# A lead with its mask loaded third, its queries in four loads, and its value sums by streaming columns

## The chip, the cores and the metric

The kernel runs on one core of a Trainium2 chip. The metric is the device time of one execution, in microseconds; of several runs the median is given. A core has TensorE (PE in the profile, its weight loads PEld), VectorE (DVE), ScalarE (ACT), GpSimd (POOL) and SyncE (SP), which here issues all DMAs.

## The reference

Local attention with block summaries, then two feed-forward layers, all in float32:

```python
k_sum = k.reshape(B, H, nb, block, D).max(axis=3)      # B 2, H 8, S 768, D 64; block 32, nb 24
v_sum = v.reshape(B, H, nb, block, D).mean(axis=3)
scores_l = where(|i - j| < 16, q @ k.T / sqrt(D), -1e9)
scores_s = q @ k_sum.T / sqrt(D) + log(block)
a = softmax(concat([scores_l, scores_s]))
x = a @ concat([v, v_sum])                             # -> 1536 x 512
h = relu(x @ w_in);  x = (h * h) @ w_out               # 512 -> 2048 -> 512
h = x @ w_in2;       return silu(h) @ w_out2
```

## The kernel before

Attention is done in 24 tiles of 64 queries (12 for each of the two batches), for all 8 heads at once, two heads to a product. A tile sees 96 keys (its window) and 24 block summaries, so 120 columns. The feed-forward layers split each float32 operand into a high and a low part and multiply three times. The first layer runs over three blocks of 512 tokens, that is of 8 tiles; the first block can start when tiles 0 to 7, the **lead**, are through attention. Tiles 8 to 15 and 16 to 23 go beside the products of the blocks.

In the first block the order of all engines but GpSimd is written by a planner, `first_order` (line 64): a list of operations, each with engine, duration, due time and what it needs. At each step it takes the operation that can start first, and on that engine, of those that can start by then, the one with the smallest due. Loads are ordered by due alone. The durations in it are the author's; the orders that come out are fixed in the program, and each engine then runs its list in that order, waiting where an operand is late.

The names of the lead's operations, which the steps below use:

- `kt`, `q`, `cst`, `vr`, `vl`: loads on SyncE of the keys (4, a head pair each), the queries (2, four tiles each), the mask with an identity matrix, the value rows (3) and the values by windows (2). `raw` loads a chunk of weights.
- `ksum` (VectorE) takes the block maxima of a head pair's keys, `kwl` (ScalarE) and `ksl` (VectorE) copy windows and maxima side by side.
- `psl` (TensorE) makes the scores of one tile and head pair, `ttl` (VectorE, line 441) adds the mask and takes the minimum, `exl` (ScalarE, line 446) the exponential with its sum; `ze`, `rc`, `nt` (VectorE, lines 466 to 477) normalise the tile; `psa` (TensorE, line 483) transposes it, `a` copies it to SBUF: on VectorE for the tiles in AVEC, on ScalarE for the others.
- `vs` (TensorE) sums the value rows in blocks, by six products into one bank, psv: the weights are a 128x24 slice of `share` (1/32 at the rows of a block), the rows stream with 512 columns. `vmean` (ScalarE, twice) copies the 24x512 means from that bank behind the windows of four tiles each (vlead).
- `av` (TensorE) multiplies two tiles' probabilities with their values, `xh` (ScalarE) and `xl` (VectorE) write the high and low part of the result. `highs` and `gemm1` 0 are the first large product; they need all four `xh`, the last also all four `xl`.
- `sc`, `sh`, `st2`, `hi`, `lo` decode a chunk of weights on ScalarE and VectorE.

Dummy matmuls (`turn`, on idle_in) are issued ten at the start (WARM), and behind the scores of tile 3: six after its first head pair, four after its second (`FILL`, line 49). The planner's durations do not count them.

Of the kernel before, what the change touches and what calls it, by code (L numbers as in the profile page):

```python
# [53 lines left out]
NMIXED = 2  # L54
PSS_AT = (1, 5, 9, 13)
PSA_AT = (3, 7, 11, 14)
AVEC = (5, 6, 7)
FIRST2 = 1
DEC1 = 14
LEADX = range(0, NLEAD, 2)  # L60
# [9 lines left out]
def first_order():  # L70
# [6 lines left out]
    def op(eng, name, arg, dur, due, deps=(), bank=(), kb=0):  # L77
        o = index[name, arg] = dict(eng=eng, name=name, arg=arg, dur=dur, due=due + shift.get(name, 0), deps=list(deps), bank=bank, kb=kb,
                                    n=len(ops))
        ops.append(o)  # L80
# [17 lines left out]
        return 24 + 7 * s  # L98


    for i, (name, arg, kb) in enumerate([("kt", 0, 393), ("q", 0, 524), ("kt", 1, 393), ("cst", 0, 250), ("kt", 2, 393),
                                         ("kt", 3, 393), ("q", 1, 524), ("vr", 0, 524), ("vr", 1, 524), ("vr", 2, 524),
                                         ("vl", 0, 1150), ("vl", 1, 1150)]):
        load(name, arg, kb, -100 + i)
    for hp in range(NHP):
        op("vec", "ksum", hp, 1.0, -50 + hp, [("kt", hp, 0)])
# [1 line left out]
            op("act", "kwl", (hp, i), .5, -50 + hp + 51 * i, [("kt", hp, 0)])  # L108
            op("vec", "ksl", (hp, i), .13, -50 + hp + 48 * i, [("ksum", hp, 0)])
    for c in range(6):  # L110
        op("pe", "vs", c, .92, 2.7 + .1 * c, [("vr", c // 2, 0)])
    for i in range(NLEAD // NGRP):
        op("act", "vmean", i, 1.9, -5, [("vs", c, M) for c in range(6)] + [("vl", i, 0)] * 0)
    for i in range(NVF):
        op("act", "vfm", i, .6, tile_due(NLEAD) - 10 + i, [("vmean", 0, 0), ("xh", LEADX[-1], 0)])

# [10 lines left out]
    for g in range(NFIRST):  # L127
        due, two = tile_due(g), g - 2 >= NLEAD
        if g < NLEAD:
            for hp in range(NHP):  # L130
                op("pe", "psl", (g, hp), .29, due, [("kwl", (hp, g // NGRP), A), ("ksl", (hp, g // NGRP), A), ("q", g // NGRP, 0)] +
                   [("psl", (g, hp - 1), 0)] * (hp > 0), bank=[] if hp else [("acc", "ttl", (g, NHP - 1))])
                op("vec", "ttl", (g, hp), .21, due, [("psl", (g, hp), M), ("cst", 0, 0)])
                op("act", "exl", (g, hp), .385, due, [("ttl", (g, hp), A)])
            exp = [("exl", (g, hp), A) for hp in range(NHP)]
        else:
            load("kw", g, 246, due - 9, [pss(g - 2) + (M,)] * two)
            load("qr", g, 131, due - 8.9, [("qd", g - 2, A)] * two)
            load("vf", g, 196, due - 6, [av(g - 2) + (M,)] * two)
            op("vec", "kwc", g, .13, due - .5, [("kw", g, 0)] + [("kvr", 2 * NHP - 1, 0)] * (g >= TPB))  # L140
            if TPB <= g < TPB + NVF:
                op("vec", "vfc", g, .35, due, [("vf", g, 0), ("vendc", 0, A)])
            op("pool", "qd", g, .72, due - 5, [("qr", g, .1)] + [pss(g - 2) + (M,)] * two)
            if g == NLEAD:
                op("pe", "vis", g, 1.95, due, [("gemm1", 1, 0), ("kwc", g, A), ("qd", g, A)], bank=[("att", "ttr", g, g + 1)])
            elif g % 2 == 0:
                op("pe", "vis", g, 3.1, due, values(g - 2) + values(g - 1) + [("kwc", g, A), ("qd", g, A)],
                   bank=[("h", "xl", g - 2), ("att", "ttr", g, g + 1)])
            else:
                index["vis", g - 1]["deps"] += [("kwc", g, A), ("qd", g, A)]  # L150
            op("vec", "ttr", g, .84, due, [pss(g) + (M,)] + [psa(g - 2) + (M,)] * two)
            op("act", "exp", g, 1.54, due, [("ttr", g, -.45)])
            exp = [("exp", g, A)]
        op("vec", "ze", g, .09, due, exp)
        op("vec", "rc", g, .1, due, [("ze", g, .1)])
        op("vec", "nt", g, .78, due, [("rc", g, .1)])
        if g < NLEAD:
            op("pe", "psa", g, .62, due - 2, [("nt", g, -.1)], bank=[("att", "a", g)])
        elif g % 2 == 0:
            op("pe", "psa", g, .85, due - 2, [("nt", g, -.1)], bank=[("att", "a", g, g + 1)])  # L160
        else:
            index["psa", g - 1]["deps"] += [("nt", g, -.1)]
        op("vec" if g in AVEC else "act", "a", g, .65 if g in AVEC else .56, due, [psa(g) + (M,)] + [av(g - 2) + (M,)] * (g >= NLEAD + 2))
        if g < NLEAD and g % 2:
            op("pe", "av", g - 1, 1.15, due, [("vl", g // NGRP, 0), ("vmean", g // NGRP, A), ("a", g - 1, A), ("a", g, A)],
               bank=[("acc", "xl", g - 1)])
            op("act", "xh", g - 1, .6, due, [("av", g - 1, M)])
            op("vec", "xl", g - 1, .7, due, [("xh", g - 1, A)])
        elif g % 2:
            if g == NFIRST - 1:  # L170
                op("pe", "av", g - 1, 1.3, due, values(g - 1) + values(g), bank=[("h", "xl", g - 1)])
            op("act", "xh", g - 1, .6, due, [av(g) + (M - 1.8 * (g < NFIRST - 1),)])
            op("vec", "xl", g - 1, .7, due, [("xh", g - 1, A)])
# [71 lines left out]
def kernel(  # L245
# [32 lines left out]
    def mm(o, l, r, **kw):  # L278
        pe.matmul(o, l, r, **kw)  # L279

    def copy(eng, o, i, scale=1.0):
        if eng is act:
            return act.activation(out=o, in_=i, func=AF.Copy, scale=scale)  # L283
        return eng.tensor_copy(out=o, in_=i)  # L284
# [88 lines left out]


    share_p = ctx.enter_context(tc.tile_pool(name="share_p", bufs=1, side="right"))
    share = share_p.tile([P, PHASE - 8], F32, tag="share", name="share")
    att_ctx = ExitStack()
    cp = att_ctx.enter_context(tc.tile_pool(name="cp", bufs=1, side="right"))
    p1 = att_ctx.enter_context(tc.tile_pool(name="p1", bufs=1, side="right"))
# [14 lines left out]

    pool.memset(share, 0.0)
    for j in range(P // KBLK):
        pool.memset(share[j * KBLK:(j + 1) * KBLK, NSUM - P // KBLK + j:NSUM - P // KBLK + j + 1], 1.0 / KBLK)
    st = {}

    def summaries(b, sums, tag):  # L400
# [234 lines left out]
    def first_block():  # L635
# [3 lines left out]

        idle_in = wi_p.tile([P, 512], F32R, tag="wi", name="idle_in")  # L640
        idle_out = ps_h.tile([P, 512], F32, tag="h", name="idle_out")
        psv = ps_h.tile([P, DM], F32, tag="h", name="psv0")
        vec.memset(idle_in.bitcast(F32), 0.0)
        early = first_p.tile([P, 1], F32, tag="early", name="early")
        act.activation(out=early, in_=idle_in[:, 0:1].bitcast(F32), func=AF.Exp)
# [18 lines left out]
            sp.dma_start(out=kts[hp][:, WIN:], in_=kT[0, hp])  # L664

        def q(i):
            gr = slice(i * NGRP, i * NGRP + NGRP)
            sp.dma_start(out=qrlead[i], in_=qW[gr].rearrange("g e d n -> (e d) g n"))

        def cst_(_):  # L670
            sp.dma_start(out=cst_sb[:, 0:3 * NK + P], in_=cst)
# [35 lines left out]
            turn(FILL.get(ghp, 0))  # L707

        def vs(c):
            lo = NSUM - P // KBLK - c * (P // KBLK)  # L710
            mm(psv[NWIN:NK], share[:, lo:lo + NSUM], vrows[c // 2][:, c % 2], start=(c == 0), stop=(c == S // P - 1))

        def vmean(i):
            means = psv[NWIN:NK]
            copy(act, vlead[NWIN:NK, i * NGRP:i * NGRP + NGRP].rearrange("p g h d -> p g (h d)"),
                 bass.AP(means.tensor, means.offset, [means.ap[0], [0, NGRP], means.ap[1]]))

# [101 lines left out]
        def psa(g):  # L819
            for i in (g,) if g < NLEAD else (g, g + 1):  # L820
                transposes(i)

        do = dict(kt=kt, q=q, cst=cst_, vr=vr, vl=vl, ksum=ksum_, kwl=kwl, ksl=ksl, vs=vs, vmean=vmean, vfm=vfm, kv=kv, kvr=kvr,
                  vend=vend, vendc=vendc, vfc=vfc, kw=kw_load, qr=q_load, vf=v_load, kwc=k_sums, qd=side_by_side,
                  vis=vis, ttr=minima, exp=exps, ze=guard, rc=inverse, psl=psl, ttl=lambda a: minimum(*a),
                  exl=lambda a: exponential(*a), nt=lambda g: norm(g, vec),
# [393 lines left out]
```

## Time and profile before

| | us |
|---|---|
| median of 3 runs | 583.91 (583.61 to 584.04) |
| the profiled execution | 583.73 |
| its span, first to last instruction | 581.9 |
| first large product starts (chain) | 34.91 |
| TensorE busy | 574.5 (99%) |
| VectorE, ScalarE busy | 386.4 (66%), 360.1 (62%) |

The profile is of one execution. Times in it count from the first instruction. Each group of instructions stands with the line of kernel.py that made it, which may be a helper's (279 is the matmul helper, 283 the copy on ScalarE, 284 that on VectorE), so tiles tell more than lines. The granted clock is TensorE's, 1.00 for full speed.

### The profile page before, as it was taken

How to read it: one execution, taken by the hardware profiler on the slowest of the kernel's cores; microseconds unless marked ns; L12 is line 12 of the kernel's file. 1: busy time of each engine (PE TensorE's matmuls, PEld its weight loads, DVE VectorE, ACT ScalarE, POOL GpSimd, SP SyncE). 2: the span in 40 equal slices, each digit the busy share in tenths (PEclk: the TensorE clock that was granted, in tenths of full speed). 3: DMA queues.
4: the chain of work that ended last, by engine and by line, in shares of the span. 5: the costliest groups of instructions: out<-in, count | busy, mean ns of one | idle time of the engine just before them, and what ended most of it. 6: DMA issues, size and time to landing. Idle time of an engine off the chain costs nothing.

```text
span 581.9 us, 9507 instructions
## 1 busy us (share of the span) xinstructions
PE 574.5 (99%) x3300; PEld 489.5 (84%) x3300; DVE 386.4 (66%) x966; ACT 360.1 (62%) x834; POOL 93.0 (16%) x101
## 2 busy tenths in 40 slices
PE   8999999999999999999999999999999999999997
PEld 6578888888888888888888889999988988889995
DVE  5999899953955765286454778666665666666641
ACT  5999878864646545376544677565555655555541
POOL 0010100102654452175332200000000000000000
PEclk9999999999999999999999999999999999999999
DMA  8999989755998879345880111242258411111002
GB/s 317 310 267 330 316 296 333 241 212 168 295 339 289 298 245 364 122 134 160 313 262 2 38 54 73 90 146 90 91 169 338 146 37 37 36 37 37 27 12 108
DMA packets 42240, 104.42 MB, mean 179 GB/s; under 512 B 4560, under 2 KB 11856, under 8 KB 42192
## 3 DMA queue, kind: packets, MB, share of 16 engines
q1 hardware_dynamic: 42192, 103.81, 52.7%
q8 instruction: 26, 0.43, 0.3%
q14 instruction: 22, 0.18, 0.1%
HBM read 78.37 MB, written 25.43 MB: 178 GB/s over the span
## 4 chain that ended last, share of the span: by engine, by line
PE 96%; ACT 2%; DMA 1%; DVE 1%; SPq 0%; issue 0%; DVEq 0%
PE acc L279 45%; PE h L279 23%; PE hx L279 12%; PE hz L279 6%; PE pss L279 3%; PE hy L279 3%; PE psa L483 2%; PE av L279 1%; DMA t_ksum<-in_kT_dram 1%; PE psv L279 1%; ACT vlead L283 1%; ACT T L446 0%; ACT xt L283 0%; PE idle_out L279 0%; DVE ksum L684 0%; DVE T L441 0%
## 5 line engine op out<-in xcount | busy, mean ns | idle before, releaser
L279 PE MATMUL h<-xt,wi 128*128 128x512 f32 x576 | 139.8, 392 | 1.0 <-ACT xt L283 1.0
L279 PE MATMUL acc<-g,wo 128*128 128x512 f32 x576 | 139.5, 391 | 0.0
L279 PE MATMUL acc<-wq,g 128*128 128x512 f32 x576 | 134.3, 390 | 0.0
L279 PEld LDWEIGHTS h<-xt,wi 128*128 128x128 f32 x576 | 107.1, 188 | 23.9 <-ACT xt L283 1.1
L279 PEld LDWEIGHTS acc<-g,wo 128*128 128x128 f32 x576 | 107.6, 188 | 22.6 <-issue 0.5
L279 PEld LDWEIGHTS acc<-wq,g 128*128 128x128 f32 x576 | 107.8, 188 | 21.9 <-DVE wq L287 0.3
L287 DVE TENSOR_TENSOR g<-r,g 128x512 fp32r<-128x512 f32 x48 | 38.8, 807 | 66.0 <-ACT g L283 40.1
L287 DVE TENSOR_TENSOR r_s<-v,r_s 128x256 fp32r<-128x256 f32 x48 | 20.3, 426 | 64.7 <-ACT r_s L283 64.7
L283 ACT ACTIVATE e<-hx 128x384 f32<-128x384 f32 x32 | 15.7, 492 | 60.4 <-PE hx L279 60.4
L446 ACT ACTIVATE T<-T,m 128x120 f32<-128x120 f32 x96 | 36.6, 382 | 7.0 <-DVE m L441 6.9
L283 ACT ACTIVATE g<-s 128x384 fp32r<-128x384 f32 x64 | 32.9, 516 | 10.5 <-DVE s L287 10.4
L279 PE MATMUL hx<-x_t,r_s 128*128 128x384 f32 x192 | 38.5, 335 | 0.0
L287 DVE TENSOR_TENSOR g<-s,g 128x384 fp32r<-128x384 f32 x64 | 35.3, 555 | 2.7 <-ACT g L283 1.1
L279 PEld LDWEIGHTS hx<-x_t,r_s 128*128 128x128 f32 x192 | 33.8, 188 | 0.3
L1032 ACT ACTIVATE s<-e 128x384 f32<-128x384 f32 x48 | 25.1, 523 | 8.4 <-DVE e L287 7.1
L284 POOL COPY qd<-qr 128x256 f32<-128x256 f32 x16 | 12.0, 767 | 111.0 <-PE pss L279 68.2
L287 POOL TENSOR_TENSOR wo<-c_wo,wo 128x512 fp32r<-128x512 f32 x16 | 25.9, 1619 | 19.2 <-ACT wo L283 18.7
L588 ACT ACTIVATE r<-h 128x512 f32<-128x512 f32 x16 | 9.6, 597 | 30.9 <-PE h L279 30.9
L592 ACT ACTIVATE r<-h 128x512 f32<-128x512 f32 x16 | 9.5, 593 | 30.6 <-PE h L279 30.6
L287 DVE TENSOR_TENSOR s<-e,s 128x384 f32<-128x384 f32 x48 | 26.4, 551 | 0.3 <-ACT s L1032 0.3
L287 POOL TENSOR_TENSOR r<-r 128x512 f32<-128x512 f32 x16 | 16.6, 1040 | 49.3 <-ACT g L593 38.1
L477 DVE TENSOR_SCALAR T<-T,r 128x120 f32<-128x120 f32 x96 | 24.2, 316 | 0.5
(112 smaller groups left out, 905.8 us busy)
## 6 DMA issues: line engine op xcount, KB each, us to landing
raw_wi<-in_w_in_dram SPq DMA_DIRECT2D x16, 512.0 KB, 5.0
raw_wo<-in_w_out_dram SPq DMA_DIRECT2D x16, 512.0 KB, 5.4
raw_wp<-in_w_out_dram SPq DMA_DIRECT2D x16, 512.0 KB, 4.9
split<-wo SPq DMA_DIRECT2D x16, 512.0 KB, 3.8
raw_wj<-in_w_in_dram SPq DMA_DIRECT2D x16, 512.0 KB, 4.7
wo<-split SPq DMA_DIRECT2D x16, 512.0 KB, 3.6
c<-scr_dram SPq DMA_DIRECT2D x32, 256.0 KB, 2.8
scr_dram<-c_wo SPq DMA_DIRECT2D x16, 256.0 KB, 3.7
```

The costliest lines, as they stand in the source:

```text
L279: pe.matmul(o, l, r, **kw)
L283: return act.activation(out=o, in_=i, func=AF.Copy, scale=scale)
L284: return eng.tensor_copy(out=o, in_=i)
L287: return eng.tensor_tensor(out=o, in0=a, in1=b, op=op)
L446: act.activation(out=d["T"][:, c], in_=d["T"][:, c], func=AF.Exp, bias=d["m"][:, c:c + 1], scale=-1.0, accum_out=d["z"][:, c:c + 1])
L477: st["norm"] = vec.tensor_scalar(out=T[:, c], in0=T[:, c], scalar1=r[:, c:c + 1], scalar2=None, op0=ALU.mult)
L483: pe.transpose(ps[0:NK, c], d["T"][:, c], id_sb)
L588: act.activation(out=r, in_=h, func=AF.Relu)
L592: act.activation(out=r, in_=h, func=AF.Relu)
L1032: act.activation(out=s, in_=src, func=AF.Sigmoid)
```

## The change

The mask is loaded third, behind the first keys and the first queries. The queries come in four loads of two tiles each; the last two stand between the loads of the value rows. The value sums are turned around: the value rows become the weights, by head pairs, and four columns of `share`, now one 128x4 pattern, stream; each of the six products writes four columns of the transposed sums. `vsc`, new, copies them (128 x 4 x 24) to SBUF on ScalarE; `vst`, new, brings them with the identity into the old layout, in a PSUM bank of its own; `vmean` reads that bank. Tile 4's `a` goes from ScalarE to VectorE. Durations and dues of these operations in the planner change with them, and so the orders that it writes; the load list has two entries more, and its dues are -100 plus the place in the list, beside -90 for the first chunk of weights.

```diff
--- before.py
+++ after.py
@@ -54,7 +54,7 @@
 NMIXED = 2
 PSS_AT = (1, 5, 9, 13)
 PSA_AT = (3, 7, 11, 14)
-AVEC = (5, 6, 7)
+AVEC = (4, 5, 6, 7)
 FIRST2 = 1
 DEC1 = 14
 LEADX = range(0, NLEAD, 2)
@@ -98,9 +98,9 @@
         return 24 + 7 * s
 
 
-    for i, (name, arg, kb) in enumerate([("kt", 0, 393), ("q", 0, 524), ("kt", 1, 393), ("cst", 0, 250), ("kt", 2, 393),
-                                         ("kt", 3, 393), ("q", 1, 524), ("vr", 0, 524), ("vr", 1, 524), ("vr", 2, 524),
-                                         ("vl", 0, 1150), ("vl", 1, 1150)]):
+    for i, (name, arg, kb) in enumerate([("kt", 0, 393), ("q", 0, 262), ("cst", 0, 250), ("kt", 1, 393), ("q", 1, 262),
+                                         ("kt", 2, 393), ("kt", 3, 393), ("vr", 0, 524), ("q", 2, 262), ("vr", 1, 524),
+                                         ("q", 3, 262), ("vr", 2, 524), ("vl", 0, 1150), ("vl", 1, 1150)]):
         load(name, arg, kb, -100 + i)
     for hp in range(NHP):
         op("vec", "ksum", hp, 1.0, -50 + hp, [("kt", hp, 0)])
@@ -108,9 +108,11 @@
             op("act", "kwl", (hp, i), .5, -50 + hp + 51 * i, [("kt", hp, 0)])
             op("vec", "ksl", (hp, i), .13, -50 + hp + 48 * i, [("ksum", hp, 0)])
     for c in range(6):
-        op("pe", "vs", c, .92, 2.7 + .1 * c, [("vr", c // 2, 0)])
-    for i in range(NLEAD // NGRP):
-        op("act", "vmean", i, 1.9, -5, [("vs", c, M) for c in range(6)] + [("vl", i, 0)] * 0)
+        op("pe", "vs", c, .47, 1.4 + .1 * c, [("vr", c // 2, 0)])
+    op("act", "vsc", 0, .3, 0.9, [("vs", c, M) for c in range(6)])
+    op("pe", "vst", 0, .9, -4, [("vsc", 0, A)])
+    op("act", "vmean", 0, 1.9, 1.6, [("vst", 0, M)])
+    op("act", "vmean", 1, 1.9, 1.8, [("vst", 0, M)])
     for i in range(NVF):
         op("act", "vfm", i, .6, tile_due(NLEAD) - 10 + i, [("vmean", 0, 0), ("xh", LEADX[-1], 0)])
 
@@ -128,7 +130,7 @@
         due, two = tile_due(g), g - 2 >= NLEAD
         if g < NLEAD:
             for hp in range(NHP):
-                op("pe", "psl", (g, hp), .29, due, [("kwl", (hp, g // NGRP), A), ("ksl", (hp, g // NGRP), A), ("q", g // NGRP, 0)] +
+                op("pe", "psl", (g, hp), .29, due, [("kwl", (hp, g // NGRP), A), ("ksl", (hp, g // NGRP), A), ("q", g // 2, 0)] +
                    [("psl", (g, hp - 1), 0)] * (hp > 0), bank=[] if hp else [("acc", "ttl", (g, NHP - 1))])
                 op("vec", "ttl", (g, hp), .21, due, [("psl", (g, hp), M), ("cst", 0, 0)])
                 op("act", "exl", (g, hp), .385, due, [("ttl", (g, hp), A)])
@@ -373,7 +375,7 @@
 
 
     share_p = ctx.enter_context(tc.tile_pool(name="share_p", bufs=1, side="right"))
-    share = share_p.tile([P, PHASE - 8], F32, tag="share", name="share")
+    share = share_p.tile([P, PHASE - 8], F32, tag="share", name="share")[:, 0:P // KBLK]
     att_ctx = ExitStack()
     cp = att_ctx.enter_context(tc.tile_pool(name="cp", bufs=1, side="right"))
     p1 = att_ctx.enter_context(tc.tile_pool(name="p1", bufs=1, side="right"))
@@ -394,7 +396,7 @@
 
     pool.memset(share, 0.0)
     for j in range(P // KBLK):
-        pool.memset(share[j * KBLK:(j + 1) * KBLK, NSUM - P // KBLK + j:NSUM - P // KBLK + j + 1], 1.0 / KBLK)
+        pool.memset(share[j * KBLK:(j + 1) * KBLK, j:j + 1], 1.0 / KBLK)
     st = {}
 
     def summaries(b, sums, tag):
@@ -639,7 +641,7 @@
 
         idle_in = wi_p.tile([P, 512], F32R, tag="wi", name="idle_in")
         idle_out = ps_h.tile([P, 512], F32, tag="h", name="idle_out")
-        psv = ps_h.tile([P, DM], F32, tag="h", name="psv0")
+        psv = ps_h.tile([P, NHP, NSUM], F32, tag="h", name="psv0")
         vec.memset(idle_in.bitcast(F32), 0.0)
         early = first_p.tile([P, 1], F32, tag="early", name="early")
         act.activation(out=early, in_=idle_in[:, 0:1].bitcast(F32), func=AF.Exp)
@@ -664,8 +666,8 @@
             sp.dma_start(out=kts[hp][:, WIN:], in_=kT[0, hp])
 
         def q(i):
-            gr = slice(i * NGRP, i * NGRP + NGRP)
-            sp.dma_start(out=qrlead[i], in_=qW[gr].rearrange("g e d n -> (e d) g n"))
+            lo = 2 * i % NGRP
+            sp.dma_start(out=qrlead[2 * i // NGRP][:, lo:lo + 2], in_=qW[2 * i:2 * i + 2].rearrange("g e d n -> (e d) g n"))
 
         def cst_(_):
             sp.dma_start(out=cst_sb[:, 0:3 * NK + P], in_=cst)
@@ -707,11 +709,21 @@
             turn(FILL.get(ghp, 0))
 
         def vs(c):
-            lo = NSUM - P // KBLK - c * (P // KBLK)
-            mm(psv[NWIN:NK], share[:, lo:lo + NSUM], vrows[c // 2][:, c % 2], start=(c == 0), stop=(c == S // P - 1))
+            n = P // KBLK
+            for hp in range(NHP):
+                mm(psv[:, hp, c * n:(c + 1) * n], vrows[c // 2][:, c % 2, hp * P:(hp + 1) * P], share, start=True, stop=True)
+
+        def vsc(_):
+            vsumT[0] = first_p.tile([P, NHP, NSUM], F32, tag="vsumT0", name="vsumT0")
+            copy(act, vsumT[0], psv)
+
+        def vst(_):
+            ps = st["vst"] = ps_h.tile([P, NHP, P], F32, tag="h", name="pst0")
+            for hp in range(NHP):
+                mm(ps[NWIN:NK, hp], vsumT[0][:, hp], id_sb, start=True, stop=True)
 
         def vmean(i):
-            means = psv[NWIN:NK]
+            means = st["vst"][NWIN:NK].rearrange("p c d -> p (c d)")
             copy(act, vlead[NWIN:NK, i * NGRP:i * NGRP + NGRP].rearrange("p g h d -> p g (h d)"),
                  bass.AP(means.tensor, means.offset, [means.ap[0], [0, NGRP], means.ap[1]]))
 
@@ -820,7 +832,7 @@
             for i in (g,) if g < NLEAD else (g, g + 1):
                 transposes(i)
 
-        do = dict(kt=kt, q=q, cst=cst_, vr=vr, vl=vl, ksum=ksum_, kwl=kwl, ksl=ksl, vs=vs, vmean=vmean, vfm=vfm, kv=kv, kvr=kvr,
+        do = dict(kt=kt, q=q, cst=cst_, vr=vr, vl=vl, ksum=ksum_, kwl=kwl, ksl=ksl, vs=vs, vsc=vsc, vst=vst, vmean=vmean, vfm=vfm, kv=kv, kvr=kvr,
                   vend=vend, vendc=vendc, vfc=vfc, kw=kw_load, qr=q_load, vf=v_load, kwc=k_sums, qd=side_by_side,
                   vis=vis, ttr=minima, exp=exps, ze=guard, rc=inverse, psl=psl, ttl=lambda a: minimum(*a),
                   exl=lambda a: exponential(*a), nt=lambda g: norm(g, vec),
```

## Rows read from the trace of the kernel before

**Rows 1.** The page, busy time of each engine, share of the span, instructions.

```profile
PE 574.5 (99%) x3300; PEld 489.5 (84%) x3300; DVE 386.4 (66%) x966; ACT 360.1 (62%) x834; POOL 93.0 (16%) x101
```

**Rows 2.** Busy time by stretches: stretch, its length, each engine's busy time (instructions), granted clock, DMA share, GB/s.

```profile
0.00:6.00 6.00, 4.54 (x10) 3.14 (x10) 1.77 (x4) 2.42 (x4) 0.92 (x13) 1.00 0.69 234
...
13.75:27.76 14.01, 13.84 (x108) 7.89 (x105) 13.46 (x91) 13.67 (x59) 0.00 (x0) 1.00 1.05 304
27.76:34.91 7.15, 5.59 (x138) 4.77 (x137) 5.90 (x16) 6.85 (x9) 1.27 (x2) 1.00 0.99 303
...
34.90:60.00 25.10, 25.09 (x137) 20.69 (x138) 24.51 (x71) 22.92 (x51) 1.25 (x2) 1.00 0.89 305
```

**Rows 3.** The chain that ended last, 0 to 46 us: start, length, what.

```profile
17.35 0.58 PE psa L483 x4
...
25.31 2.70 PE psv L279 x6
...
28.04 3.63 ACT vlead L283 x2
...
33.86 0.51 ACT wi L283
34.36 0.50 ACT xt L283
...
34.91 5.74 PE h L279 x24
```

**Rows 4.** ScalarE's groups by form, 0 to 35 us: busy, mean ns of one, idle before.

```profile
L446 ACT ACTIVATE T<-T,m 128x120 f32<-128x120 f32 x32 | 12.2, 382 | 1.1 <-DVE m L441 1.0
...
L283 ACT ACTIVATE vlead<-psv 24x2048 f32<-24x2048 f32 x2 | 3.6, 1863 | 0.3 <-PE psv L279 0.3
```

**Rows 5.** Order of time, ScalarE and VectorE: start, length, engine, line, tiles, count.

```profile
16.80 0.57 ACT L283 ACTIVATE a<-psa 120x512 f32<-120x512 f32 x1
...
17.27 0.38 ACT L446 ACTIVATE T<-T,m 128x120 f32<-128x120 f32 x1
...
30.12 0.69 DVE L284 COPY a<-psa 120x512 f32<-120x512 f32 x1
```

**Rows 6.** Order of time, TensorE's small products and their weight loads.

```profile
17.28 0.41 PEld L483 LDWEIGHTS psa<-cst_sb,T 128*120 128x120 f32 x4
17.28 0.65 PE L483 MATMUL psa<-cst_sb,T 128*120 128x128 f32 x4
...
21.28 1.90 PE L279 MATMUL psv<-vrows,share 128*24 128x512 f32 x4
...
29.96 3.95 PE L279 MATMUL av<-a,vlead 120*64 120x64 f32 x128 [0.31 <-ACT vlead L283]
```

**Rows 7.** Order of time, the start of the lead.

```profile
1.46 4.63 PE L279 MATMUL idle_out<-idle_in 128*128 128x512 f32 x10 [1.46 <-DVE idle_in L643]
...
6.02 1.31 PE L279 MATMUL pss<-kws,qrlead 64*64 64x120 f32 x16
...
7.25 1.64 PE L279 MATMUL idle_out<-idle_in 128*128 128x512 f32 x6
...
9.06 0.39 ACT L446 ACTIVATE T<-T,m 128x120 f32<-128x120 f32 x1 [0.56 <-DVE m L441]
...
9.17 1.59 PE L279 MATMUL pss<-kws,qrlead 64*64 64x120 f32 x16 [0.28 <-DVE m L441]
...
10.12 0.95 DVE L684 TENSOR_REDUCE ksum<-t_ksum 128x24 f32<-128x768 f32 x1
...
11.83 4.03 PE L279 MATMUL pss<-kws,qrlead 64*64 64x120 f32 x60
...
13.75 0.40 ACT L446 ACTIVATE T<-T,m 128x120 f32<-128x120 f32 x1 [0.49 <-DVE m L441]
```

**Rows 8.** The mask's load: its issue in order of time, its time to landing.

```profile
2.19 0.43 SPq L671 DMA_DIRECT2D cst_sb<-in_cst_dram  x1
...
DMA to landing us min/median/max: 6.0/6.0/6.0
```

## The prediction

> **What bounds the kernel now.** I read the page first. TensorE is busy 574.5 us [rows 1] of a span of 581.9 us, so the hope lies where it is not doing the large products. The busy time by stretches [rows 2] says where that is: from 34.90 us on TensorE is busy 25.09 of 25.10 us, and no wait of TensorE is listed behind that point. All that a change of the lead can bring is an earlier start of the first large product, which stands at 34.91 us in the chain [rows 3]; call that time S. What comes later in the lead makes the kernel longer by as much, what comes earlier makes it shorter, as long as the decoding behind S keeps up.
>
> Then the chain from 0 to 46 us, and beside it the same stretches engine by engine. The chain shows TensorE up to 28.01 us (its last piece there is six value-sum matmuls), the two `vmean` copies for 3.63 us on ScalarE, and then the `xh` copies [rows 3]. Read alone, this says that the value sums are late and the copies of the means lie bare on the path. The stretches say something else [rows 2]: from 13.75 to 27.76 us (the end of the last lead exponential) ScalarE is busy 13.67 of 14.01 us, VectorE 13.46, TensorE 13.84, and from 27.76 to 34.91 us ScalarE is again busy 6.85 of 7.15. **ScalarE has 0.64 us of holes between 13.75 us and S.** Moving a copy on it from behind the exponentials to between them makes nothing shorter; only work taken off ScalarE, holes closed, or an earlier start of its solid stretch do.
>
> **The change part by part.**
>
> Value sums. Removed: 12 matmuls of 512 columns, 4 in 1.90 us [rows 6], or some 5.5 us in all. Added: 6 sums of 4 products, two instructions each as float32 shows, so 48 with a load of 128 columns and 4 streamed ones; and `vst`, 8 instructions that stream 128 columns. No row shows a full load with so short a stream. The nearest ends: `av`, loads and streams of 64 columns, 128 in 3.95 us, 0.031 us each; `psa`, loads of 120 and streams of 128 columns, 4 in 0.58 us by the chain [rows 3], 0.145 each. In `psa` the loads follow one another sooner, 4 in 0.41 us, the last lasting 0.137: 0.091 each [rows 6]. The 48 cost 1.5 to 7.0 us. I take `av`'s rate scaled from 64 to 128 columns, 0.062, so 0.5 us a sum and 3.0 us in all, since `psa`'s spacing can be its stream and not its load. `vst` I put at 1.1 us by `psa` (8 x 0.145).
>
> Does this lie beside other work? In the new dues the sums stand at 1.4 to 1.9, so between the scores of tiles 5 and 7; by my walk through the planner's rule the first two fill gaps in which TensorE waits for normalised tiles, the last four stand behind tile 6's scores, and the last two behind tile 7's. The fourth tile's transposes end at 21.2 us by that walk (tile 0 normalised at 16.8, one tile each 1.25 us behind it on VectorE, then 0.6 of transposes); then come six score pairs of tiles 6 and 7 at 4 x 0.067 us (60 in 4.03 us [rows 7]), 1.6 us, and the four sums. They end at about 22.8 us + 4c, where c is the cost of one: 24.8 us for c = 0.5. ScalarE reaches `vsc` at 24.9 us (below). So the sums hide, with 0.1 us to spare.
>
> The Trainium skill speaks against this part: its page "TensorE: Matmul & The Clock Gate", section "LDWEIGHTS (loading the stationary operand)", gives a load as columns divided by 1.2 in ns, 107 ns for 128. By it, an estimate, the 48 loads take 5.1 us, the sums end at 26.2 us, and ScalarE would stand. No row here shows a bare load.
>
> ScalarE's list. The `vmean` copies (1.863 us each [rows 4], 1.82 by the chain's 3.63 for two) stay. Their dues 1.6 and 1.8 put the first ahead of tile 7's last two exponentials and the second right behind them. Added: `vsc`, 128x96 from PSUM, between 0.09 (`a`'s 0.47 us for 512 columns [rows 5], scaled to 96) and 0.382 us (the 128x120 exponential with its sum [rows 4]); I take 0.3, by the nearer shape. Removed: tile 4's `a`, 0.47 us from its start to the next start (16.80 to 17.27 us shows the like [rows 5]). It goes to VectorE at 0.69 us [rows 5], which has 14.01 - 13.46 = 0.55 us of holes in that stretch [rows 2], so it fills them; if it pushed tile 7's normalisation, 0.1 to 0.2 us would come back, which I leave in the range.
>
> Mask third, queries split. The bytes before the second queries' landing are 384 + 256 + 244 + 384 + 256 = 1524 KB, just what lay before the mask in the old order (384 + 512 + 384 + 244), which was issued at 2.19 us and landed 6.0 us later [rows 8]: tiles 2 and 3 can be scored from 8.2 us, not from 6.02 with the rest [rows 7]. Tiles 0 and 1 are scored at 6.02, and with the mask there their first two exponentials (0.77 us) run in a hole of ScalarE, ahead of 9.06 us, where the first stood [rows 7]. But six dummy matmuls are issued behind tile 3's first scores (the FILL table). They lay at 7.25 to 8.89 us, under the wait for the second keys [rows 7]. Now they begin at 8.8 us and hold TensorE to 10.2 (six at 0.24 us, as 24 such products took 5.74 [rows 3]), so the second pair's scores start there and not at 9.17. VectorE's list has tile 0's second minimum ahead of the third key maximum, which moves from 10.12 [rows 7] to 10.7 us, and everything up to 13 us by some 0.8. ScalarE loses at the end of this what it won: in the old order its 7th exponential started at 13.75 us behind a 0.49 us wait [rows 7], in the new one I get 13.65 us with six done as well. Worth 0.10 us; between nothing and 0.77 by whether those dummies hold.
>
> The load order behind that. By the planner's dues the first weight chunk (-90) now goes ahead of the last value rows (-89) and the value windows. The last value rows and the value windows land 512 KB later, 1.7 us at the 304 GB/s of that stretch [rows 2], so by the bytes ahead of them near 18 and 21 us, before their uses at 23.7 and 28 us. Cost nothing; if not, the sums wait and rival 2's price holds. The two added loads cost SyncE about 0.43 us each at issue [rows 8], while the transfers ahead of them still run.
>
> **The sum.** Old: 14.01 us from 13.75 to the last exponential, then 7.15 us to S. New last exponential: 13.65 + 14.01 - 0.47 + 0.30 + 1.82 (first `vmean` ahead of it) = 29.31 us; `vsc` starts 0.30 + 6 x 0.382 + 1.82 = 4.4 earlier, 24.9 us. Behind it 7.15 - 0.28 (wait for the sums, gone) - 3.63 + 1.82 = 5.06 us, so S = 34.37. **That is 0.54 us earlier: -0.10 early, -0.47 + 0.30 on ScalarE's list, -0.28 of wait.** What is late next: tile 7. From the last exponential to its `a` took 27.76 to 30.81 us [rows 2, 5], 3.05 us, so 32.36; then one `av` (3.95/4 = 1.0 us [rows 6]), one `xh` (0.5 [rows 3]) and hand-overs of some 0.2: 34.1 us. The two paths end 0.3 us apart. The profiled execution took 583.73 us, 1.83 us more than its span; less 0.54 it is 583.2. The median of the runs is 583.91, 0.18 above it; less 0.54 that is 583.4 us.
>
> **The rivals.**
> 1. More comes through. The dummies do not hold the lists (the 0.77 us of early exponentials stay won, 0.67 more than taken), and the second chunk's copy, 0.51 us on the old chain [rows 3], falls behind S. S = 34.37 - 1.18 = 33.2, but tile 7's path then ends at 34.1 - 0.67 = 33.4: 1.5 us gained, 582.4 us; at the most favourable, with the value rows' hand-overs short, 582.2. For it: VectorE and ScalarE have work ready; against: the lists are in order.
> 2. **Slower: the loads lie bare.** Place: the last four value sums, and `vsc` at ScalarE's head with tile 6's and 7's exponentials queued behind it, so tile 7's normalisation and `xh` behind those. S = 34.37 + (22.8 + 4c + 0.1 - 24.9). At 0.091 us an instruction (c = 0.73) this is 35.3 us, at 0.145 (c = 1.16) 37.0 us: 584.3 to 586.0 us. It passes the old S from c = 0.64, 0.08 us an instruction. For it: `psa`'s spacing; against: `av`'s 0.031. By the figure of the Trainium skill's page named above, S would be about 35.8 us (an estimate).
> 3. Slower: TensorE's clock. The first ten dummies go out at 0.46 us each, later ones at 0.27 [rows 7], by their level 1.2 and 2.4 GHz, though the granted clock reads 1.00 from the start [rows 2]. The wait for the second queries leaves TensorE idle from 6.6 to 8.2 us, where it was busy. Should it fall back, ten dummies cost up to 0.2 us more each, 2 us, of which some 0.5 lies under VectorE's key maxima: about 1.5 us, 584.9 us. No row shows a hole of that size, so it has a small chance.
> 4. Nothing moves: tile 4's `a` on a full VectorE takes back ScalarE's gain, 583.9 us.
>
> **How the numbers follow.** A measurement of this kernel tells 0.2% (1.17 us) from no change. Forecast (gain 0.1 to 1.1): 0.40, within. Rival 1: 0.25, faster. Rival 2: 0.20, half of it (c above 0.93) over the bound. Rival 3: 0.10, slower. Rival 4: 0.05, within. Faster 0.25, same 0.40 + 0.10 + 0.05 = 0.55, slower 0.10 + 0.10 = 0.20. The range goes from rival 1's 582.2 to 585.2, which takes in most of rival 2 (c up to about 0.96) and rival 3's middle; left out are rival 2's worst end and rival 3's.
>
> **What would show it.** S in the chain at 34.1 to 34.6 us, and TensorE without a wait behind it. Step by step: the six dummies behind 8.8 us and the second scores at about 10.1; the 7th exponential at about 13.65; 48 value-sum matmuls at near 0.06 us, the last ending by 24.9; no wait of ScalarE for the sums; one `vmean` ahead of tile 7's last exponentials. Wrong would make it: a wait of ScalarE at `vsc` (rival 2), dummies at 0.43 us each (rival 3), ScalarE's 7th exponential at 13.0 or earlier (rival 1), or idle time of TensorE behind S, which would mean that an earlier start isn't fed.

## The result and the profile after

The changed kernel takes **589.16 us** (median of four, 588.55 to 591.18) against 583.80 us of the kernel before on the same chip (583.61 to 584.04): the ratio is 1.0098, with a 95% interval from 1.0073 to 1.0122. It is slower by 5.4 us, 4.0 us above the upper end of the range that was forecast.

The page's busy times, to be held against [rows 1], and all waits of TensorE in the profiled execution of 588.55 us (span 586.7 us): engine, line, waited for, us, times, longest.

```profile
PE 579.2 (99%) x3344; PEld 497.5 (85%) x3344; DVE 385.5 (66%) x967; ACT 360.9 (62%) x834; POOL 94.1 (16%) x101
```

```profile
PE idle_out L281 <- DVE idle_in L645: 1.5, 1, 1.5
PE pss L281 <- DMA qrlead<-in_qW_dram: 1.0, 1, 1.0
PE h L281 <- ACT xt L285: 0.7, 1, 0.7
PE av L281 <- ACT vlead L285: 0.4, 1, 0.4
PE pss L281 <- DVE m L443: 0.2, 1, 0.2
```

TensorE is busy 4.7 us longer, and the span is 4.8 us longer. None of the five waits lies behind the first large product; the third is the wait that ends in it. So the first statement of the prediction holds: the time is set by S, the start of that product. The chain of work that ended last (start, length, what) puts S at 39.58 us where it was 34.91 [rows 3], 4.67 us later:

```profile
21.76 0.58 PE psa L485 x4
22.34 0.67 PE pss L281 x8
23.01 1.88 PE psv L281 x16
24.89 1.15 PE pss L281 x16
26.04 3.23 PE psv L281 x16
29.27 0.95 PE psa L485 x4
30.21 1.85 PE pst L281 x8
32.06 0.02 issue
32.08 1.87 ACT vlead L285
...
39.58 5.78 PE h L281 x24
```

The last four value sums stand on the path in two lots of 16 instructions, and the second lot takes 3.23 us where the first takes 1.88. The `vst` products behind them (`pst`) take 1.85 us. ScalarE in order of time, with its idle time in brackets, shows who waits:

```profile
29.30 0.25 ACT L285 ACTIVATE vsumT<-psv 128x96 f32<-128x96 f32 x1 [3.31 <-PE psv L281]
...
32.08 1.87 ACT L285 ACTIVATE vlead<-pst 24x2048 f32<-24x2048 f32 x1 [1.02 <-PE pst L281]
```

ScalarE stands 3.31 us at `vsc` with tile 6's and 7's exponentials queued behind it, and another 1.02 us at the first `vmean`. The busy time by stretches of the same execution (stretch, length, each engine, granted clock, DMA share, GB/s) says why the second lot is longer:

```profile
25.00:26.00 1.00, 1.00 (x17) 0.89 (x17) 0.16 (x1) 0.99 (x6) 0.00 (x0) 1.00 1.04 414
26.00:27.00 1.00, 1.00 (x9) 1.00 (x7) 0.91 (x9) 0.00 (x0) 0.00 (x0) 0.66 0.99 397
27.00:30.00 3.00, 3.00 (x15) 2.80 (x15) 0.69 (x4) 0.70 (x4) 0.00 (x0) 0.50 1.09 381
30.00:33.00 3.00, 3.00 (x14) 2.17 (x14) 2.71 (x9) 1.98 (x7) 1.29 (x2) 0.50 1.07 235
33.00:34.00 1.00, 0.61 (x5) 0.37 (x3) 0.88 (x2) 0.97 (x2) 0.00 (x0) 0.93 0.92 351
```

TensorE is busy all the time from 25 to 33 us, and still its granted clock falls to 0.50, the 1.2 GHz level, in the last lot of sums. In the old kernel it was 1.00 in the stretches shown of the lead [rows 2].

So three things can have cost the 4.67 us: the sums' own time on TensorE, the clock behind them, and what the split loads do early. The experiments separate them.

### The profile page after: what moved, and what is told of

Its sections match the earlier page's. It is cut to its first block, busy times and chain, and to the rows that moved or that the text cites. A ratio compares the mean times of both kernels' runs of the same rounds, so it can differ in the third digit from the quotient of the medians.

```text
span 586.7 us, 9597 instructions
## 1 busy us (share of the span) xinstructions
PE 579.2 (99%) x3344; PEld 497.5 (85%) x3344; DVE 385.5 (66%) x967; ACT 360.9 (62%) x834; POOL 94.1 (16%) x101
## 4 chain that ended last, share of the span: by engine, by line
PE 96%; ACT 1%; DMA 1%; DVE 1%; SPq 0%; issue 0%; DVEq 0%
PE acc L281 45%; PE h L281 23%; PE hx L281 11%; PE hz L281 6%; PE pss L281 4%; PE hy L281 3%; PE psa L485 2%; PE av L281 1%; PE psv L281 1%; DMA qrlead<-in_qW_dram 1%; ACT vlead L285 1%; ACT xt L285 0%; PE pst L281 0%; DVE ksum L686 0%; PE idle_out L281 0%; ACT T L448 0%
## 5 line engine op out<-in xcount | busy, mean ns | idle before, releaser
L285 ACT ACTIVATE g<-s 128x384 fp32r<-128x384 f32 x64 | 32.9, 517 | 10.2 <-DVE s L289 10.1
L479 DVE TENSOR_SCALAR T<-T,r 128x120 f32<-128x120 f32 x96 | 25.7, 331 | 0.3
L443 DVE CUSTOM_DVE_ANT_0 T<-pss,cst_sb 128x120 f32<-128x120 f32 x96 | 21.6, 276 | 5.6 <-PE pss L281 5.5
```

Source lines behind the costliest of these rows:

```text
L443: vec.tensor_tensor_reduce(out=d["T"][:, c], in0=d["ps"][:, c], in1=cst_sb[:, kind * NK:kind * NK + NK], scale=-0.125, scalar=3.0e38, op0= ...
L479: st["norm"] = vec.tensor_scalar(out=T[:, c], in0=T[:, c], scalar1=r[:, c:c + 1], scalar2=None, op0=ALU.mult)
```

## The experiments

Medians in us; the kernel before, timed on the same chip beside each, is in the last column.

| run | what it is | median (lowest to highest, count) | ratio (95%) | before |
|---|---|---|---|---|
| e1_loads_only | before + the loads' new order | 586.34 (584.56 to 586.66, 9) | 1.0033 (1.0024 to 1.0043) | 583.98 |
| e2_sums_only | before + the new value sums | 590.24 (589.23 to 590.79, 4) | 1.0105 (1.0089 to 1.0120) | 583.98 |
| e4_a_moved | before + tile 4's `a` on VectorE | 584.05 (583.60 to 584.62, 10) | 1.0001 (0.9992 to 1.0011) | 583.98 |
| e5_fill_moved | e1 with six dummies moved | 583.90 (583.48 to 584.19, 10) | 0.9999 (0.9989 to 1.0008) | 584.03 |
| e3_wide_stream | after, 64 columns streamed | 587.64 (586.80 to 589.20, 4) | 1.0057 (1.0040 to 1.0074) | 583.98 |
| e11_after_fill | after with six dummies moved | 588.48 (587.10 to 588.63, 4) | 1.0078 (1.0064 to 1.0093) | 584.04 |
| e6_both_cured | after, 64 columns, dummies moved | 585.58 (584.62 to 586.36, 10) | 1.0029 (1.0019 to 1.0039) | 584.03 |
| e7_true_price | e6, the planner told the sums' price | 586.25 (586.02 to 586.45, 4) | 1.0039 (1.0024 to 1.0054) | 584.03 |
| e10_half_loads | e6 with half of the sums | 582.93 (582.20 to 583.83, 10) | 0.9982 (0.9973 to 0.9992) | 584.03 |
| e12_rows_added | e5, pairs of value rows added on GpSimd | 584.74 (583.61 to 586.92, 12) | 1.0014 (1.0004 to 1.0025) | 584.04 |

**The three parts alone.** The loads (with the queries' dependency on `g // 2`), the sums (with `vsc`, `vst` and the `vmean` dues), and `AVEC` were each put into the kernel before:

```diff
-    for i, (name, arg, kb) in enumerate([("kt", 0, 393), ("q", 0, 524), ("kt", 1, 393), ("cst", 0, 250), ...
+    for i, (name, arg, kb) in enumerate([("kt", 0, 393), ("q", 0, 262), ("cst", 0, 250), ("kt", 1, 393), ...   # e1
...
+                mm(psv[:, hp, c * n:(c + 1) * n], vrows[c // 2][:, c % 2, hp * P:(hp + 1) * P], share, start=True, stop=True)   # e2
...
-AVEC = (5, 6, 7)
+AVEC = (4, 5, 6, 7)   # e4
```

> The kernel before with only the loads of the change: mask third, queries in four loads, and what that does to the planner's orders; value sums and tile 4's a as before. Theory A (the streaming value sums cost the time, by bare weight loads and by a lower clock behind them): within 0.6 us of the kernel before, 583.2 to 584.4 us, the dummies behind tile 3's first scores at 8.4 us as after the change. Theory C (the loads cost it: TensorE's wait for the second queries and the displaced dummies delay every list): 585 us or more.

> The kernel before with only the new value sums (four streaming columns, vsc, vst, their dues); loads and tile 4's a as before. Theory A: 587.5 to 589.5 us, value-sum matmuls at 0.12 us each while the clock is full, 0.2 us each once the granted clock reads 0.50, ScalarE waiting for the sums for 2 us or more ahead of vsc. Theory C: 584 to 585 us, the clock stays at 1.00.

> The kernel before with only tile 4's a moved from ScalarE to VectorE. Every theory: within 0.5 us of the kernel before, 583.3 to 584.3 us, since the value sums and vmean set the end of the lead there; the move by itself buys nothing as long as ScalarE waits for the sums.

The sums alone cost 6.3 us, more than Theory A's range allowed, the loads 2.4, as Theory C said, the moved `a` nothing. In e2 S stands at 41.69 us; its last two sums take 3.50 us, and the granted clock is 0.50 from 28 to 35 us, as in the changed kernel. None of the parts gains, and they do not add up to the 5.4 us of the whole: in e2's profiled execution (590.79 us, the longest of its four) the first 64 instructions of `av` run at the fallen clock too, 3.68 us where the changed kernel's take 2.09. For e4 one line of ScalarE says where the 0.47 us went:

```profile
27.67 3.63 ACT L283 ACTIVATE vlead<-psv 24x2048 f32<-24x2048 f32 x2 [1.12 <-PE psv L279]
```

Off ScalarE's list, the copy became a longer wait for the old value sums, 1.12 us where 0.28 was. From the start of ScalarE's solid stretch to the end of the sums both profiles take 14.26 us (13.39 to 27.65 us here, 13.75 to 28.01 before). ScalarE was not the only engine that bound the stretch. That S stays (34.97 against 34.91 us) has a second reason: the 0.36 us by which this execution was ahead are lost again behind the copies, mostly where ScalarE waits for VectorE's part of a weight chunk, which takes 1.20 us beside two GpSimd copies and 0.68 in the profile of before.

```profile
31.93 1.29 POOL L284 COPY qd<-qr 128x256 f32<-128x256 f32 x2 [30.30 <-DMA qr<-in_qW_dram]
...
32.57 1.20 DVE L334 SCALAR_TENSOR_TENSOR c_wi<-c_wi,raw_wi 128x512 int32<-128x512 int32 x1
...
33.80 0.63 ACT L283 ACTIVATE wi<-c_wi 128x512 fp32r<-128x512 f32 x1 [0.31 <-DVE c_wi L334]
```

**The early hole.** In the changed kernel TensorE's order of time shows the wait for the second queries, and the six dummies behind it:

```profile
7.73 0.74 PE L281 MATMUL pss<-kws,qrlead 64*64 64x120 f32 x8 [1.04 <-DMA qrlead<-in_qW_dram]
8.40 1.67 PE L281 MATMUL idle_out<-idle_in 128*128 128x512 f32 x6
10.00 1.22 PE L281 MATMUL pss<-kws,qrlead 64*64 64x120 f32 x16
```

e1's nine executions fall into two groups: three at 584.56 to 585.11 us with a mean granted clock of 1.000, six at 586.29 to 586.66 us with 0.997. To test the hole, e5 issues the six dummies behind the first scores of tile 1, ahead of the second queries:

```diff
-FILL = {(NGRP - 1, 0): 6, (NGRP - 1, 1): 4}
+FILL = {(1, 0): 6, (NGRP - 1, 1): 4}
```

> e1 (only the loads of the change) with the six dummy matmuls moved from behind tile 3's first scores to behind tile 1's, where TensorE waits for the second queries. Theory H (that wait lets the clock fall in most executions, and the dummies behind it hold the second scores back): clock 1.00 in nearly all executions, second scores at about 8.7 us and not 9.9, 583.2 to 584.2 us, no executions at 586. Rival (something else in the load order, as the later value rows or the planner's new order): 584.5 us or more with executions at 586 again.

```profile
6.04 1.66 PE L279 MATMUL idle_out<-idle_in 128*128 128x512 f32 x6
8.17 1.87 PE L279 MATMUL pss<-kws,qrlead 64*64 64x120 f32 x24 [0.47 <-DMA qrlead<-in_qW_dram]
```

This is e5's TensorE: the dummies fill the hole, the second pair's scores start in the group at 8.17 us and not at 10.00, and all ten executions lie between 583.48 and 584.19 us with a clock of 0.999 or more. This is Theory H. The loads without the hole cost nothing, and gain nothing: e5 equals the kernel before, though the fill brings its chain 1.07 us ahead of e1's at the scores of 12.54 (13.61) us.

**The stream's width.** e3 streams 64 columns in each sum (the pattern and zeros) where the change streams 4; the weight loads stay the same. The width of the psv tile and the columns that `vsc` copies follow from it and are not shown.

```diff
-    share = share_p.tile([P, PHASE - 8], F32, tag="share", name="share")[:, 0:P // KBLK]
+    share = share_p.tile([P, PHASE - 8], F32, tag="share", name="share")[:, 0:64]
...
-                mm(psv[:, hp, c * n:(c + 1) * n], vrows[c // 2][:, c % 2, hp * P:(hp + 1) * P], share, start=True, stop=True)
+                mm(psv[:, hp, c * n:c * n + 64], vrows[c // 2][:, c % 2, hp * P:(hp + 1) * P], share, start=True, stop=True)
```

> The changed kernel with 64 columns streamed in each value-sum matmul instead of 4 (60 of them zeros that the next sum overwrites): same 48 loads, same order, same count. Theory A1 (short streams let the clock fall): the granted clock stays at 1.00, each matmul still takes about 0.12 us behind its load, the first large product starts at 36 to 37 us, 585.5 to 587 us. Theory A2 (the clock falls for the bare loads whatever streams): clock 0.50 from 26 us again, 588.5 to 591 us.

Streaming sixteen times as much makes the kernel faster, by 1.5 us in the medians, though the two ranges overlap. The time lies above A1's range and below A2's. e3's profiled execution (589.20 us) has its clock fall elsewhere, in the early hole, as its TensorE and the stretches beside it show:

```profile
8.48 1.08 PE L281 MATMUL pss<-kws,qrlead 64*64 64x120 f32 x8 [2.40 <-DMA qrlead<-in_qW_dram]
9.49 2.93 PE L281 MATMUL idle_out<-idle_in 128*128 128x512 f32 x6
```

```profile
6.00:11.80 5.80, 3.40 (x16) 2.52 (x14) 2.36 (x11) 3.10 (x11) 0.00 (x0) 0.66 1.05 391
...
16.60:25.00 8.40, 8.40 (x92) 7.21 (x88) 7.80 (x56) 7.26 (x29) 0.00 (x0) 1.00 1.06 252
25.00:35.00 10.00, 9.06 (x89) 7.69 (x89) 7.59 (x44) 7.75 (x30) 1.22 (x2) 1.00 1.01 325
```

There the hole is 2.40 us long (the second queries' load ends at 8.44 us, in the changed kernel's profile at 7.68), and six dummies take 2.93 us where they took 1.67. Amid the value sums, 16.60 to 35.00 us, the clock stays at 1.00, as A1 said. So two runs take the `FILL` line over: e11 the change with it alone, e6 with 64 columns as well. They differ in nothing but the streamed width.

> The changed kernel with only the six dummy matmuls moved into the wait for the second queries; the value sums stream 4 columns as in the change. It differs from e6 (585.6 us) by the 64 columns alone. Theory K (the short streams let the clock fall amid the value sums): clock 0.50 for some us from about 25 us on, though the start of the lead is as in e6; 587.3 to 588.8 us. Rival (the clock fell there only because the early hole had left TensorE behind): clock 1.00, 585.2 to 586 us.

> The changed kernel with both clock losses taken away: 64 columns streamed in each value-sum matmul and the six dummies moved into the wait for the second queries. Clock 1.00 throughout. Theory L (bare loads of 0.12 us remain, 48 of them, and ScalarE stands for them ahead of vsc): 585.8 to 587 us, ScalarE's wait at vsc 1.5 us or more. Rival (the clock was all of it): 584.5 us or less.

e11's TensorE and its stretches:

```profile
21.71 1.95 PE L281 MATMUL psv<-share,vrows 128*128 128x4 f32 x16
...
24.73 2.43 PE L281 MATMUL psv<-share,vrows 128*128 128x4 f32 x16
...
28.04 1.90 PE L281 MATMUL pst<-cst_sb,vsumT 128*24 128x128 f32 x8
```

```profile
21.30:28.04 6.74, 6.74 (x60) 6.16 (x59) 4.04 (x29) 4.30 (x22) 0.00 (x0) 0.85 1.04 325
28.04:31.70 3.66, 3.66 (x17) 2.69 (x16) 2.59 (x10) 2.64 (x7) 0.00 (x0) 0.50 1.07 326
```

The same of e6:

```profile
21.28 2.00 PE L281 MATMUL psv<-share,vrows 128*128 128x64 f32 x16
...
24.36 2.00 PE L281 MATMUL psv<-share,vrows 128*128 128x64 f32 x16
...
26.73 1.05 PE L281 MATMUL pst<-cst_sb,vsumT 128*24 128x128 f32 x8
```

```profile
26.40 0.25 ACT L285 ACTIVATE vsumT<-psv 128x96 f32<-128x96 f32 x1 [2.06 <-PE psv L281]
```

```profile
21.30:28.04 6.74, 6.74 (x65) 6.14 (x64) 4.79 (x35) 4.68 (x26) 0.00 (x0) 1.00 1.03 340
28.04:31.70 3.66, 2.72 (x62) 2.23 (x61) 2.63 (x10) 3.59 (x8) 0.00 (x0) 1.00 1.08 317
```

Sixteen instructions take 1.95 us with 4 columns and 2.00 with 64: **the stream does not set the pace of 0.12 us**. That the load of 128 columns sets it is inferred, since no run varied the load's width; a fixed cost of every instruction it is not, as `av`'s follow one another at 0.031 us [rows 6]. TensorE is busy 6.74 of 6.74 us in both, but behind the short streams the clock falls to 0.50 and `pst` takes 1.90 us, with the wide ones it stays at 1.00 and `pst` takes 1.05. All four executions of e11 have a mean clock of 0.991 to 0.994, all ten of e6 0.999 or more. This is Theory K. The difference is worth 588.48 - 585.58 = 2.9 us, and the two kernels' times do not overlap. Why short streams let the clock fall is not shown.

**What is left.** e6 is still 1.6 us behind the kernel before, a little less than Theory L's range had it, and ScalarE waits 2.06 us at `vsc`. e7 tells the planner what a sum takes, in case only the order was wrong (`vsc` ahead of work that was ready):

```diff
-        op("pe", "vs", c, .47, 1.4 + .1 * c, [("vr", c // 2, 0)])
+        op("pe", "vs", c, .98, 1.4 + .1 * c, [("vr", c // 2, 0)])
```

> e6 with one number changed in the planner: a value sum is priced at 0.98 us, as measured, and not 0.47. Its list puts vsc behind tile 7's third exponential and not amid tile 6's. If the exponentials queued behind the waiting vsc are what costs, 1 us or more below e6; if the sums' own time on TensorE is what costs, within 0.8 us of e6 or above it.

It gains nothing (586.25 us): in its chain the last two sums start 2.45 us later than e6's, both `vmean` copies follow them bare, 3.64 us as in the old kernel, and S is 37.13 us (e6: 35.67). The exponentials queued behind `vsc` are not the cost, or moving them ahead of it would gain; but that order has a price of its own, the bare copies, so e7 alone does not say that the sums' time is the cost. e10 takes TensorE's work away instead: it sums head pairs 0 and 1 alone, 24 products for 48, and copies their columns into the places of pairs 2 and 3, whose sums it leaves out.

```diff
-            for hp in range(NHP):
+            for hp in range(NHP // 2):
```

> e6 with the value sums of head pairs 2 and 3 left out (those of pairs 0 and 1 are copied in their place), so 24 loads and not 48, all else and the order the same. Theory L: TensorE's part shrinks by 24 x 0.12 = 2.9 us, the wait at vsc goes, 583.6 to 584.8 us. Rival (the rest of the lead, vst or vmean amid the exponentials, sets the end): within 0.8 us of e6.

```profile
23.13 1.10 PE L281 MATMUL psv<-share,vrows 128*128 128x64 f32 x8
...
33.55 4.65 PE L281 MATMUL h<-xt,wi 128*128 128x512 f32 x19 [0.70 <-ACT xt L285]
```

```profile
24.27 0.25 ACT L285 ACTIVATE vsumT<-psv 128x96 f32<-128x96 f32 x1 [0.27 <-PE psv L281]
```

With 24 instructions fewer, 2.9 us of TensorE at 0.12, the kernel gains more than Theory L's range allowed: it is 2.65 us faster than e6 and 1.1 us faster than the kernel before. ScalarE waits 0.27 us at `vsc` where e6's waits 2.06, and S is 33.55 us. The saving comes through almost one to one: the sums lie on the path.

**A version with less TensorE work.** If TensorE's list is what costs, fewer products of the old form should gain. e12 adds the two value rows of a partition on GpSimd first, so that three products of 512 columns (two instructions each) do for six; there is no `vsc` or `vst`. For this the value rows are loaded so that the two rows of a partition belong to one block, and the pattern comes with the mask's load (not shown).

```diff
+        op("pool", "vadd", c, 1.1, c, [("vr", c, 0)])
+        op("pe", "vs", c, .92, 1.4 + .1 * c, [("vadd", c, A)])
...
+            tt(pool, vrows[c][:, 0], vrows[c][:, 0], vrows[c][:, 1], ALU.add)
```

> e5 (loads of the change, dummies in the wait) with tile 4's a on VectorE, vmean dues as in the change, and the value sums halved in the old form: GpSimd, idle in the lead, adds the two value rows that a partition holds, and three products of 512 columns sum them (the pattern of ones comes with the mask's load). No vsc, no vst. Theory L (TensorE's time for the sums is what ScalarE waits for, and 2.75 us less of it lets ScalarE's list run through): first large product at 33.2 to 33.9 us as in e10, 582.3 to 583.2 us. Rival (TensorE is not what counts in the old form, since e10 gained by vsc's earlier means): 583.6 to 584.4 us.

It takes 584.74 us, 0.7 us more than the kernel before, with 2.75 us less on TensorE. Both ranges missed it. GpSimd's and VectorE's order of time (profiled execution of 586.92 us):

```profile
11.74 1.28 POOL L288 TENSOR_TENSOR vrows<-vrows 128x512 f32<-128x512 f32 x1 [4.88 <-DMA vrows<-in_vP_dram]
...
19.14 1.31 POOL L288 TENSOR_TENSOR vrows<-vrows 128x512 f32<-128x512 f32 x1 [4.09 <-DMA vrows<-in_vP_dram]
```

```profile
12.25 0.83 DVE L285 COPY kws<-ksum 128x96 f32<-128x96 f32 x1
...
15.75 0.20 DVE L285 COPY kws<-ksum 128x96 f32<-128x96 f32 x1
...
18.08 0.85 DVE L476 TENSOR_SCALAR T<-T,r 128x120 f32<-128x120 f32 x4
...
19.25 1.86 DVE L476 TENSOR_SCALAR T<-T,r 128x120 f32<-128x120 f32 x4
```

Under a GpSimd addition the copy takes 0.83 us for 0.20, and the four normalising products take 1.86 for 0.85. The copy ends as the addition does (13.08 against 13.02 us); of the products three are left when the third addition ends (20.45 us), and in the chain they start at 20.46. The Trainium skill says on its page "SBUF — State Buffer", section "Terms", that VectorE and GpSimd arbitrate for a shared port pair, which one of them holds for a whole instruction while the loser is blocked; these rows agree. It did not hit every instruction: beside the second addition (13.77 to 15.05 us) the minimum of the scores takes 0.28 us as elsewhere. In this execution the granted clock is also down, at 0.52 from 28 to 35 us. Of the twelve executions the eight with a clock of 1.000 take 583.61 to 584.80 us, the four with less 585.13 to 586.92: even without the loss of clock it doesn't beat the kernel before. None of the eight was profiled, so what holds them back is open. No version that computes all of the sums beat the kernel before.

## Why the prediction was wrong

**The size of c: the step that failed.** The forecast took 0.062 us for a sum instruction, `av`'s rate scaled by columns, so c = 0.5 us. The trace after shows sixteen in 1.88 us, 0.12 each: c = 0.94 us at full clock, between rival 2's two prices (0.73 and 1.16), and 1.6 us in the last lot at the fallen clock, above both ends. The Trainium skill's page "TensorE: Matmul & The Clock Gate", section "LDWEIGHTS (loading the stationary operand)", whose rule gives 107 ns for 128 columns (an estimate), was much nearer than the forecast; the rows show 118 to 122. What was wrong in choosing: `av`'s 0.031 us, scaled from 64 to 128 columns, is half of what was measured, so its rate does not carry over by columns (no run shows why), and `psa`'s loads, 0.091 us apart and the last 0.137 long [rows 6], were nearest in size among those with so short a stream.

**The term that was missing.** With c = 0.94 the forecast's own sum gives 585.2 us (583.4 + 4 x 0.44), the edge of its range. Of the 4.0 us that the measured time lies beyond it, 2.9 are a cost that the sum did not have: the slower clock amid and behind the value sums (e11 against e6).

**What bounds the lead.** The prediction read ScalarE's 0.64 us of holes as the bound and put the sums "beside other work". The row that it quotes [rows 2] has TensorE busy 13.84 of 14.01 us: it had 0.17 us of holes there, fewer than ScalarE's 0.34 in the same stretch (the 0.64 count on to S). What lengthens TensorE's list there lengthens the lead. The change takes 12 instructions off it (5.5 us) and puts on 48 at 0.12 (5.8) and `vst` at 1.0 (e6), 1.3 us more in all; e6 against e5, which differ by the sums and by the `a` that is worth nothing, measures 585.58 - 583.90 = 1.7 us. e10 shows the same price with the other sign. And the gain of 0.47 us from tile 4's `a` fails for the same reason: in e4 it turns into ScalarE's wait for TensorE's sums.

**The walk through the planner's rule** put two sums into gaps of TensorE. Two sums did come before the fourth tile's transposes, but not in gaps: at 14.97 and 19.61 us in the chain, with no wait of TensorE around them, 0.98 and 0.99 us. The fourth tile's transposes, forecast to end at 21.2 us, end at 22.34.

**The forecast's sum against the trace.** S came 39.58 - 34.37 = 5.2 us behind the forecast. The transposes are 1.14 us late; the six score pairs take 1.82 us for 1.6, 0.22 more; the four sums take 1.88 + 3.23 = 5.11 us for 2.0, 3.11 more, of which 1.76 is c at full clock (4 x 0.44) and 1.35 the clock; the hand-over is 0.07 shorter; and from `vsc` to S it is 10.28 us for 9.47, 0.81 more, where `psa` and `pst` run at the fallen clock. That makes 5.21 us.

**Rival 2** named the right place, the right waiter and a price close to c at full clock, but had a chance of 0.20, and its worst end, 586.0 us, held no clock. Its formula with 0.96 us (e6, 1.93 us for 16) gives 34.37 + 22.8 + 3.84 + 0.1 - 24.9 = 36.2 us; e6, whose clock stays up, has 35.67.

**Rival 3** looked for the clock in the wait for the second queries. That exists: e1's six executions with less clock are some 1.5 us longer than the three without, which is the price that rival 3 gave, and e5, which fills the hole, is 2.4 us faster than e1. But in the changed kernel's profiled execution the hole of 1.04 us left six dummies at 1.67 us, at the 2.4 GHz level. The larger fall came where no step looked, in the value sums, with TensorE busy throughout.

**The parts of the loss**, by medians from one kernel to the next: the change to e11, 0.7 us (the early hole and the dummies behind it; the two intervals overlap); e11 to e6, 2.9 us (the clock behind the short streams); e6 to e5, 1.7 us (TensorE's own time for the sums). Together 5.3 us, and e5 equals the kernel before. The split depends on the order: with 64 columns the hole is worth 587.64 - 585.58 = 2.1 us, with four 0.7. Why it is smaller there was not tested.

**What held.** S sets the time, and nothing waits behind it. The six dummies at 8.40 us and the second scores at 10.00 us (forecast 8.8 and 10.2), ScalarE's 7th exponential at 13.61 us (13.65), `vsc` at 0.25 us (0.3), `vst` at 0.98 us by e6's chain (1.1), one `vmean` ahead of tile 7's last two exponentials, no wait for the value rows or windows in their later places, and no gain of rival 1's kind.

## What to carry to other kernels

Before an addition to an engine is costed at nothing, look at that engine's holes in the very stretch, for each engine alike: two engines with 0.17 and 0.34 us of holes in 14 us both bind, and work taken off one turns into a wait for the other. Products that stream a few columns are not cheap for it: with 4 columns or 64 they took the same 0.12 us here, so replacing wide streams by many loads saves nothing where the loads are as many as here; count instructions, not columns. After such a change, read the granted clock by stretch: here half of the loss was a slower clock, on an engine that the busy times show as full.

## What the runs showed of the hardware that was not expected

- A float32 product that loads 128 columns takes 0.12 us an instruction whether it streams 4 columns or 64 (16 in 1.95 and 2.00 us), so 60 columns more cost 0.003 us each time.
- The granted clock fell to 0.50 on a TensorE that was busy 6.74 of 6.74 us, after four-column streams behind 128-column loads (e11), and stayed at 1.00 with 64 columns in the same places (e6). At the lower level the last lot took 3.23 us for 1.88 in the changed kernel.
- A wait of TensorE of about 1 us in e1's profiled execution left the clock at 1.00; one of 2.40 us in e3's came with 0.66 in its stretch (6.00 to 11.80 us). In both kernels the executions differ: e1's clock is 1.000 in three of nine, and e3's from 0.994 to 1.000 in four.
- A GpSimd addition of 128x512 in SBUF takes 1.28 us and holds a VectorE copy of 0.20 us for 0.83 (e12); a weight chunk's operation on VectorE took 1.20 us for 0.68 beside two GpSimd copies (e4).
